# Another order for the first quarter of a fused attention and gated MLP kernel

## The chip, the cores and the metric

The program runs on one core of a Trainium2 chip. A core has a matrix engine (PE, which also has a queue for loading weights, PEld), a vector engine (DVE), a scalar engine (ACT), GpSimd (POOL) and a queue engine (SP) that here only issues transfers. Each engine takes its own instructions strictly in the order in which the program lists them, and waits at the first one whose inputs are not there. The metric is the device time of one execution in microseconds (us), as the median of several runs.

## The reference

Attention with a bucket mask, and then a gated MLP without a nonlinearity:

```python
def _attn_ref(q, k, v, proj):            # q, k, v: (4, 8, 768, 64), proj: (64, 6)
    q_bits = np.einsum('bhsd,dk->bhsk', q, proj) > 0        # 6 bits per token
    k_bits = np.einsum('bhsd,dk->bhsk', k, proj) > 0
    mask = q_bucket[:, :, :, None] == k_bucket[:, :, None, :]  # buckets made of the bits
    scores = np.where(mask, q @ k.T / sqrt(64), -1e9)
    attn = softmax(scores)
    return attn @ v
def _moe_ref(x, w_a, w_b, w_out):        # x: (3072, 512), d_ff = 1536
    return ((x @ w_a) * (x @ w_b)) @ w_out
```

The output of the attention, with its heads side by side, is the x of the MLP. Everything is float32 outside; inside the kernel most products run on 16-bit pieces, a high and a low one, of the float32 numbers.

## The kernel before, in words

The four batches are worked on one after the other, and each is cut into chunks of one or two blocks of 128 tokens (14 chunks). For a chunk there are eight or sixteen "query tiles" (`qtile`): scores of 128 queries against 768 keys on PE (`s`, L1136), their maximum on DVE (`mx`, L1156), a scale and a bias made from it (`sc`, `bias`, L1164 and L1168, on DVE or POOL), the exponential on ACT (`e`, L1177), a transpose of the result, and the product with v on PE (`av`). For the first chunk the transpose is made by PE (`et`); later it is a cast, a subtraction and a transfer that transposes (`at`).

Before the scores, q and k are prepared (`split`). A product of each with itself (`gram_q`, `gram_k`, L596) gives a bound, from which a power of two is made (`ps`, L534, then `ai`, L546 and L549). With it, the input is cut into a high part (L569 on DVE or L567 on ACT) and a low part (L670, DVE). High and low are transposed (`qt`, `kt`, L688, on PE for batch 0) and copied back (`trq`, `trk`, L560). Six hash bits are then computed from the transposed parts (`qb`, `kb`, L709 on PE; `neg`, L727 on ACT; `bits`, L730 on DVE) and written as extra rows beside the data (L736, L739 into `hp`), which are transposed and copied in a second round. A score needs both rounds of its q and its k. In batch 0 there are four pairs of heads for k (`rk` 0 to 3).

The MLP's weights arrive in float32, 512 KB each transfer (`to_f32`, L855), are put into an internal form by POOL or ACT (L868, L866), ACT (L876) and DVE (L884), and a bound is taken of them too (`gram_w`, L902). The first two chunks use float32 weights (L1363), the others 16-bit halves (L1371). The products with w_a and w_b are `ab`, their gated result is `g` (L1392, L1400, L1411, L1416), the last product is `o` (L1436). `ps_cx` (L768) gives the scale of a chunk's x. MLP work of a chunk stands between the query tiles of later chunks, so that PE has work while a score goes round DVE and ACT.

No scheduler runs: the program has 3,725 operations (`op`), numbered as the code makes them, and a table `ORDER` says in which order they are issued. A second table, `ENGINE_OF`, says on which engine those run that may run on several. `Plan.issue` only follows the two. Buffers are handed out in that order too: a tile that shares a buffer waits for the readers of the tile before it. There are two PSUM buffers for scores and the transposes `qt` and `kt`, and three smaller ones.

Of the kernel before, what the change touches and what calls it, by code (L numbers as in the profile page):

```python
# [426 lines left out]
def attention_moe(ctx: ExitStack, tc: tile.TileContext, q, k, v, proj, w_a, w_b, w_out, cst, out):  # L427
# [7 lines left out]
    op = plan.op  # L435
# [37 lines left out]
    pj = cp.tile([P, NBITS], F32, tag="pj", name="pj")  # L473
# [36 lines left out]
    pw = cp.tile([P, 4], F32, tag="pw", name="pw")  # L510
# [1029 lines left out]
```

## Time and profile before

| | |
|---|---|
| median of 3 runs | 891.82 us (891.47 to 892.02) |
| profiled execution | 892.21 us, of which the span from the first to the last instruction is 890.4 us |
| PE busy | 869.0 us, 98% of the span |
| DVE, ACT, POOL busy | 631.1, 565.9, 438.0 us |
| chain that ended last | 70% of the span PE; of it L1371 35%, L1436 17%, L1136 10%, L1205 8% |
| read and written in HBM | 37.82 MB, 6.29 MB |

Busy time is the sum of the time in which an engine had an instruction. The profile names, for idle time in front of an instruction, what ended it. PE is busy nearly always, so the places where it is not busy are few, and each has its own cause.

### The profile page before, as it was taken

The numbers are of one execution on the slowest core, as the hardware profiler recorded it, in microseconds if no ns is written. First come the engines' busy times: TensorE is split into PE (matmuls) and PEld (weight loads), VectorE is DVE, ScalarE is ACT, GpSimd is POOL, SyncE is SP. The second block draws the span as 40 slices with busy tenths as digits, with TensorE's granted clock in tenths as the row PEclk, the third lists the DMA queues.
The fourth block names the chain that finished last, engine by engine and source line by source line (L and its number), as shares of the span: only waits on it lengthen the run. The fifth ranks groups of instructions, "written<-read, shape, count | busy, mean of one in ns | idle before, by whom it ended". The sixth has DMA issues, their size and how long they took to land.

```text
span 890.4 us, 24299 instructions
## 1 busy us (share of the span) xinstructions
PE 869.0 (98%) x9761; PEld 672.4 (76%) x9761; DVE 631.1 (71%) x1461; ACT 565.9 (64%) x1116; POOL 438.0 (49%) x371
## 2 busy tenths in 40 slices
PE   5899999999999999999999999999999999999998
PEld 4798777878777777777777777777777777777775
DVE  7998999988876766767776775767778576643311
ACT  6887767766657777667666675667676466644222
POOL 2444456447426556554454565545556457544111
PEclk9999999999999999999999999999999999999999
DMA  9989996899979979998977787799987666745100
GB/s 328 302 268 260 173 167 148 155 191 191 196 144 191 162 162 168 172 224 154 185 137 155 149 170 158 131 195 173 200 170 138 125 149 125 144 90 103 30 24 24
DMA packets 430433, 145.31 MB, mean 163 GB/s; under 512 B 404080, under 2 KB 422640, under 8 KB 430320
## 3 DMA queue, kind: packets, MB, share of 16 engines
q1 hardware_dynamic: 430160, 143.76, 79.5%
q8 instruction: 76, 1.25, 0.6%
q14 instruction: 37, 0.30, 0.1%
q10 hardware_dynamic: 160, 0.00, 0.0%
HBM read 37.82 MB, written 6.29 MB: 50 GB/s over the span
## 4 chain that ended last, share of the span: by engine, by line
PE 70%; DVE 3%; issue 1%; ACT 0%; DVEq 0%; ACTq 0%
PE ab L1371 35%; PE o L1436 17%; PE s L1136 10%; PE av L1205 8%; DVE vh L569 0%; DVE g L1400 0%; PE qb L709 0%; DVE mx L1156 0%; PE kb L709 0%; DVE hp L736 0%; DVE hp L739 0%; DVE ai_q L549 0%; DVE osb L569 0%; DVE kt L670 0%; PE ps_cx L768 0%
## 5 line engine op out<-in xcount | busy, mean ns | idle before, releaser
L1371 PE MATMUL ab<-xT,wz 128*128 128x256 f16 (+1 forms) x3456 | 377.2, 264 | 1.0 <-DVE g L1400 0.8
L563 POOL TENSOR_TENSOR a<-e,a 128x768 f16<-128x768 f32 x170 | 286.2, 1687 | 186.7 <-ACT a L560 84.0
L1371 PEld LDWEIGHTS <-wz 128*128 128x128 f16 x3456 | 310.4, 98 | 49.5 <-issue 1.5
L1177 ACT ACTIVATE e<-s,bias,sc 128x768 f32<-128x768 f32 x192 | 189.7, 988 | 110.3 <-DVE bias L1168 93.0
L1156 DVE TENSOR_REDUCE mx<-s 128x1 f32<-128x768 f32 x192 | 182.6, 953 | 53.2 <-PE s L1136 49.1
L1436 PE MATMUL o<-wz,g 128*128 128x512 f16 (+1 forms) x840 | 215.8, 392 | 0.2 <-DVE g L1400 0.2
L1416 POOL TENSOR_TENSOR g<-g,g 128x256 f16<-128x256 f32 x132 | 94.8, 718 | 191.1 <-ACT g L1411 185.5
L1136 PE MATMUL s<-trk,trq 76*128 76x384 f16 (+1 forms) x768 | 155.0, 327 | 2.4 <-ACT e L1177 1.8
L1400 DVE SCALAR_TENSOR_TENSOR g<-ab,ab,a 128x256 f32<-128x256 f32 x132 | 63.4, 480 | 105.1 <-ACT a L1392 87.2
L1205 PEld LDWEIGHTS <-at 128*128 128x128 f16 x3312 | 117.5, 98 | 16.5 <-issue 2.7
L1436 PEld LDWEIGHTS <-g 128*128 128x128 f16 x792 | 73.9, 98 | 68.7
L1392 ACT ACTIVATE a<-ab,ab 128x256 f32<-128x256 f32 x132 | 62.1, 470 | 99.5 <-PE ab L1371 86.6
L1205 PE MATMUL av<-vh,at 128*128 128x64 f16 x2208 | 121.9, 193 | 0.0
L1136 PEld LDWEIGHTS <-trq 76*128 76x128 f16 (+1 forms) x768 | 70.6, 98 | 44.1 <-issue 6.8
L1411 ACT CAST g<-g 128x256 f16<-128x256 f32 x132 | 53.0, 402 | 59.0 <-DVE g L1400 48.5
L560 ACT CAST a<-e 128x768 f16<-128x768 f32 x102 | 84.5, 829 | 3.0 <-DMA at<-a 1.2
L1205 PE MATMUL av<-vl,at 128*128 128x64 f16 x1104 | 62.4, 193 | 0.0
L1363 PE MATMUL ab<-xT,wz 128*128 128x128 f32 x384 | 49.4, 279 | 0.0
L560 DVE CAST a<-e 128x768 f16<-128x768 f32 x68 | 39.4, 580 | 14.0 <-ACT e L1177 14.0
L1363 PEld LDWEIGHTS ab<-xT,wz 128*128 128x128 f32 x384 | 46.2, 192 | 3.4 <-issue 2.2
L1168 DVE TENSOR_SCALAR bias<-mx,sc 128x1 f32<-128x1 f32 x181 | 38.8, 214 | 6.4
L1164 DVE TENSOR_SCALAR sc<-mx,cq 128x1 f32<-128x1 f32 x181 | 38.3, 211 | 4.8
(171 smaller groups left out, 793.7 us busy)
## 6 DMA issues: line engine op xcount, KB each, us to landing
rq<-in_q_dram SPq DMA_DIRECT2D x24, 256.0 KB, 3.5
rk<-in_k_dram SPq DMA_DIRECT2D x16, 384.0 KB, 3.9
wz<-in_moe_w_a_dram SPq DMA_DIRECT2D x12, 512.0 KB, 5.9
wz<-in_moe_w_b_dram SPq DMA_DIRECT2D x12, 512.0 KB, 5.0
wz<-in_moe_w_out_dram SPq DMA_DIRECT2D x12, 512.0 KB, 5.6
out_dram<-osb SPq DMA_DIRECT2D x24, 256.0 KB, 2.4
vr<-in_v_dram SPq DMA_DIRECT2D x12, 384.0 KB, 4.4
at<-a SPq DMA_TRANSPOSE x184, 3.6
```

The costliest lines, as they stand in the source:

```text
L560: {"ACT": nc.scalar.copy, "DVE": nc.vector.tensor_copy, "POOL": nc.gpsimd.tensor_copy}[e](out=out, in_=x)
L563: (nc.gpsimd if e == "POOL" else nc.vector).tensor_tensor(out=out, in0=x, in1=y, op=ALU.subtract)
L1136: nc.tensor.matmul(ps.t[:, jj, :HALF], lhsT=trq.t[rows, i, (2 * j + h) * nt + t], rhs=tr.t[rows, i, k0 : k0 + NT // 2].rearrange("p n s -> ...
L1156: lambda: nc.vector.tensor_reduce(out=mx.t[:, col], in_=halves(ps.t), axis=AX.XY, op=ALU.max, negate=True),
L1177: lambda: nc.scalar.activation(flat2(e.t), halves(ps.t), AF.Exp, bias=bias.t[:, col], scale=sc.t[:, col], accum_out=sm.t[:, u : u + 1],),
L1205: nc.tensor.matmul(av.t[:, u, :], lhsT=at.t[:, a + kt, :], rhs=w.t[:, h, kt, :], start=i == 0, stop=i == 3 * NT - 1,)
L1363: nc.tensor.matmul(pl.t[:, m, to], lhsT=wt32(m, cc, f), rhs=xt.t[:, cc * nt // NC, cc * nt % NC : cc * nt % NC + nt, :], start=cc == 0, st ...
L1371: nc.tensor.matmul(pl.t[:, m, to], lhsT=wt(m, wi, cc, f), rhs=xt.t[:, cc * nt // NC, xi, cc * nt % NC : cc * nt % NC + nt, :], start=i == ...
L1392: lambda a=a, pl=pl, gr=gr, sc_of=sc_of: nc.scalar.activation(a.t, pl.t[:, 0, :CH], AF.Copy, scale=sc_of(gr)),
L1400: lambda a=a, g32=g32, pl=pl, gr=gr, sc_of=sc_of: nc.vector.scalar_tensor_tensor(out=g32.t, in0=pl.t[:, 1, :CH], scalar=sc_of(gr + 1), in1 ...
L1416: lambda g=g, g32=g32, g_of=g_of: nc.gpsimd.tensor_tensor(out=g_of(g[1]), in0=g32.t, in1=g_of(g[0]), op=ALU.subtract),
L1436: nc.tensor.matmul(po[u].t.rearrange("p a b -> p (a b)"), lhsT=x()[:, us], rhs=w, start=f == 0 and i == 0, stop=f == NF - 1 and i == len(t ...
```

## The change

The first 1,100 places of `ORDER` hold the same operations in another order; behind them nothing moves. 1,078 of these places hold another operation than before. 108 operations run on another engine: 31 go from DVE to POOL, 24 from DVE to ACT, 20 from ACT to DVE, 17 from POOL to DVE, 8 from ACT to POOL and 8 from POOL to ACT. Among those from DVE to POOL are 18 pairs of scale and bias; four such pairs go back. One operation, the small constants, is given an input in the plan so that it may stand behind the loading of `proj`.

```diff
 ORDER = (
-    2, 1, 75, 11, 76, 4, 3, 77, 5, 78, 79, 80, 81, 0, 12, 13, 14, 15, 6, 282, 281, 9, 10, 84, 27, 16, 82, 17, 83, 18,
+    1, 2, 5, 11, 3, 12, 4, 75, 281, 76, 13, 77, 78, 79, 14, 15, 114, 9, 10, 80, 6, 0, 16, 27, 7, 28, 81, 17, 29, 84,
...
 ENGINE_OF = {
     "ACT": (
-        19, 20, 35, 36, 42, 58, 64, 67, 74, 83, 84, 90, 105, 107, 119, 128, 138, 140, 149, 157, 159, 166, 168, 176, 178,
+        16, 19, 20, 26, 42, 64, 74, 80, 83, 90, 107, 109, 111, 119, 121, 130, 138, 140, 147, 149, 159, 176, 178, 185, 187,
...
-    op("DVE", 0.4, pw_consts, -79, w=["pw"])
+    op("DVE", 0.4, pw_consts, -79, r=[("pj", 0), ("pj", 1)], w=["pw"])
```

The first place is PE between the first transposes of k and its second round, at 9 to 18 us of the trace. `kt_0_0` is pair 0, `kt_0_1` pair 1; loads of weights and repeats are left out. Before:

```order
L688 MATMUL kt_0_0_155<-identh,kt_0_0_140 128x128
...
L596 MATMUL gram_k_1_171<-rk_1_138 128x128
...
L534 MATMUL ps_k_1_191<-st_k_1_189,onesr 128x1
...
L709 MATMUL kb_0_199<-pjw_67,trk_0_168 128x12
...
L709 MATMUL qb_0_217<-pjw_68,trq_0_153 128x12
...
L596 MATMUL gram_k_3_235<-rk_3_233 128x128
...
L688 MATMUL kt_0_1_246<-identh,kt_0_1_212 128x128
...
L534 MATMUL ps_k_3_267<-st_k_3_242,onesr 128x1
...
L688 MATMUL kt_0_0_278<-identh,hp_77 128x128
```

And now:

```order
L688 MATMUL kt_0_0_182<-identh,kt_0_0_137 128x128
...
L596 MATMUL gram_k_3_208<-rk_3_206 128x128
...
L688 MATMUL kt_0_1_217<-identh,kt_0_1_202 128x128
...
L534 MATMUL ps_k_3_232<-st_k_3_230,onesr 128x1
...
L709 MATMUL kb_0_235<-pjw_67,trk_0_195 128x12
...
L709 MATMUL qb_0_254<-pjw_68,trq_0_180 128x12
...
L596 MATMUL gram_k_2_275<-rk_2_250 128x128
...
L688 MATMUL kt_0_0_283<-identh,hp_77 128x128
```

The hash products of pair 0 (`kb_0`, `qb_0`) now stand behind the transposes of pair 1, and a product of pair 2 stands before the second round of pair 0.

The second place is PE around the first two scores, at 19 to 29 us. Before:

```order
L688 MATMUL qt_0_0_328<-identh,hp_76 128x128
...
L534 MATMUL ps_k_2_342<-st_k_2_339,onesr 128x1
...
L534 MATMUL ps_q_0_350<-st_q_0_348,onesr 128x1
...
L688 MATMUL kt_0_1_360<-identh,hp_77 128x128
...
L1136 MATMUL s_0_0_1_0_388<-trk_0_168,trq_0_153 128x384
...
L902 MATMUL gram_w_403<-wz 128x128
...
L596 MATMUL gram_v_0_423<-v_0_346 128x128
...
L1136 MATMUL s_0_0_0_0_433<-trk_0_168,trq_0_153 128x384
...
L688 MATMUL kt_0_2_439<-identh,kt_0_2_383 128x128
```

And now:

```order
L688 MATMUL qt_0_0_345<-identh,hp_76 128x128
...
L534 MATMUL ps_k_2_354<-st_k_2_331,onesr 128x1
...
L596 MATMUL gram_v_2_361<-v_2_323 128x128
...
L534 MATMUL ps_q_0_374<-st_q_0_341,onesr 128x1
...
L1136 MATMUL s_0_0_1_0_380<-trk_0_195,trq_0_180 128x384
...
L688 MATMUL kt_0_1_395<-identh,hp_77 128x128
...
L902 MATMUL gram_w_409<-wz 128x128
...
L1136 MATMUL s_0_0_0_0_432<-trk_0_195,trq_0_180 128x384
...
L688 MATMUL kt_0_2_442<-identh,kt_0_2_388 128x128
```

A product of v stands before the first score, and the second round of pair 1 (`kt_0_1` from `hp`) has moved behind it.

The third place is ACT in the second chunk, at 74 to 84 us, around the exponential `e_0_1_1_0`; `wz` are weights on their way to the internal form. Before:

```order
L1177 ACTIVATE e_0_3_0_0_1165,sm_0_1004<-s_0_3_0_0_1087,bias_0_951,sc_0_949 128x768
L866 ACTIVATE wz<-wz 128x1024
L560 CAST a_1_0_2_1_0_1171<-e_0_2_1_0_1065 128x768
L1392 ACTIVATE a_2_1190<-ab_2_1106 128x256
L876 ACTIVATE wz<-wz 128x1024
L1177 ACTIVATE e_0_1_1_0_1249,sm_0_1004<-s_0_1_1_0_1218,bias_0_951,sc_0_949 128x768
```

And now:

```order
L1177 ACTIVATE e_0_2_1_0_1136,sm_0_938<-s_0_2_1_0_1027,bias_0_905,sc_0_903 128x768
L567 ACTIVATE qt_3_0_1144<-rq_0_720,ai_q_0_1077 128x8x64
L866 ACTIVATE wz<-wz 128x1024 x2
L1177 ACTIVATE e_0_1_1_0_1169,sm_0_938<-s_0_1_1_0_1147,bias_0_905,sc_0_903 128x768
L1392 ACTIVATE a_2_1176<-ab_2_1071 128x256
```

The weight step L876 no longer stands directly before this exponential; two earlier ones of L866 do.

## Rows read from the trace of the kernel before

**Rows 1.** The page: span, and busy time of each engine.
```profile
span 890.4 us, 24299 instructions
...
PE 869.0 (98%) x9761; PEld 672.4 (76%) x9761; DVE 631.1 (71%) x1461; ACT 565.9 (64%) x1116; POOL 438.0 (49%) x371
```

**Rows 2.** Waits of PE: line <- releaser: us in total, times, longest.
```profile
PE gram_q L596 <- DMA rq<-in_q_dram: 4.0, 1, 4.0
...
PE s L1136 <- ACT e L1177: 1.8, 4, 0.6
PE ps_cx L768 <- ACT e L1177: 1.5, 1, 1.5
```

**Rows 3.** Five stretches: length, then busy us of PE, PEld, DVE, ACT, POOL, clock.
```profile
0.00:22.30 22.30, 12.30 (x133) 10.83 (x134) 16.11 (x51) 14.38 (x20) 5.14 (x8) 1.00 0.94 327
22.30:41.40 19.10, 16.88 (x186) 13.54 (x183) 18.64 (x43) 15.14 (x20) 9.20 (x9) 1.00 0.99 300
41.40:230.00 188.60, 186.19 (x2316) 152.93 (x2316) 170.69 (x364) 137.29 (x248) 97.72 (x84) 1.00 0.93 195
230.00:245.00 15.00, 13.51 (x152) 9.90 (x150) 13.57 (x29) 8.89 (x18) 7.05 (x6) 1.00 0.96 207
245.00:890.40 645.40, 640.13 (x6989) 485.21 (x6984) 412.04 (x978) 390.20 (x811) 318.88 (x264) 1.00 0.75 143
```

**Rows 4.** Timeline to 29 us: start, us, engine, instruction, [idle before].
```profile
9.66 1.46 PE L688 MATMUL kt<-identh,kt 128*128 128x128 f16 x12
...
12.50 2.18 ACT L876 ACTIVATE wz<-wz 128x1024 f32<-128x1024 f32 x2
...
12.66 0.49 PE L709 MATMUL kb<-pjw,trk 128*128 128x12 f16 x12 [0.31 <-ACT trk L560]
...
15.30 0.20 ACT L727 COPY neg_k<-kb 128x72 f32<-128x72 f32 x1
...
17.84 0.93 ACT L567 ACTIVATE kt<-rk,ai_k 128x768 f16<-128x768 f32 x1
...
18.92 0.94 DVE L560 COPY trk<-kt 128x1536 f16<-128x1536 f16 x1
...
20.82 1.01 ACT L560 COPY trq<-qt 128x1024 f16<-128x1024 f16 x1
...
21.93 1.44 PE L688 MATMUL kt<-identh,hp 128*128 128x128 f16 x12 [0.38 <-ACT trq L560]
...
23.17 1.48 PE L1136 MATMUL s<-trk,trq 76*128 76x384 f16 x4
...
24.45 1.91 PE L902 MATMUL gram_w<-wz 128*128 128x128 bf16 x16
...
28.24 0.83 PE L688 MATMUL kt<-identh,kt 128*128 128x128 f16 x12
28.91 1.08 PE L902 MATMUL gram_w<-wz 128*128 128x128 bf16 x16
```

**Rows 5.** The same columns as rows 3, for two stretches before 28 us.
```profile
16.40:21.90 5.50, 4.06 (x46) 3.76 (x46) 5.33 (x13) 5.33 (x8) 1.87 (x1) 1.00 1.01 346
21.90:28.00 6.10, 6.07 (x42) 4.79 (x43) 5.72 (x12) 4.21 (x5) 3.16 (x3) 1.00 1.02 345
```

**Rows 6.** Timeline around 82 us.
```profile
80.58 1.16 ACT L876 ACTIVATE wz<-wz 128x1024 f32<-128x1024 f32 x1 [3.44 <-DMA wz<-in_moe_w_b_dram]
...
82.75 0.81 PE L1136 MATMUL s<-trk,trq 76*128 76x384 f16 x4 [0.48 <-ACT e L1177]
```

**Rows 7.** The bias of a query tile (L1168): duration in ns, shortest/median/longest.
```profile
L1168 DVE TENSOR_SCALAR bias<-mx,sc x181: 212/214/217, 26.8 to 815.9; 128x1 f32<-128x1 f32 x181
L1168 POOL TENSOR_SCALAR bias<-mx,sc x11: 259/260/1280, 29.8 to 207.6; 128x1 f32<-128x1 f32 x11
```

**Rows 8.** The page's groups: maximum and exponential of a query tile.
```profile
L1177 ACT ACTIVATE e<-s,bias,sc 128x768 f32<-128x768 f32 x192 | 189.7, 988 | 110.3 <-DVE bias L1168 93.0
L1156 DVE TENSOR_REDUCE mx<-s 128x1 f32<-128x768 f32 x192 | 182.6, 953 | 53.2 <-PE s L1136 49.1
```

**Rows 9.** Timeline around 231 to 236 us.
```profile
231.53 1.64 POOL L563 TENSOR_TENSOR a<-e,a 128x768 f16<-128x768 f32 x1
231.54 1.69 DVE L739 TENSOR_SCALAR hp<-bits_k 128x72 f16<-128x72 f32 x1
...
235.24 0.27 PE L768 MATMUL ps_cx<-identb,cxs 128*128 128x128 bf16 x2 [1.49 <-ACT e L1177]
```

176 rows, old and new, of tables (ENGINE_OF, ORDER) are left out of this document.

## Prediction, made before the changed kernel ran

> **What bounds the kernel now.** I read the page first. PE is busy 869.0 us of a span of 890.4 us [rows 1], so whatever the change does, it can only win or lose in the 21.4 us in which PE is idle, or in PE's own speed. The profiled execution took 892.21 us, 1.8 us more than its span and 0.39 us above the median of the runs, 891.82 us; I make the sum against the profiled one and take the difference off the median.
>
> Next, the five stretches [rows 3]: length minus PE's busy time is PE's idle time. It is 10.0 us until 22.3 us, 2.22 us until 41.4 us, 2.41 us from there to 230 us, 1.49 us in the 15 us that follow, and 5.27 us in the remaining 645.4 us. The change reorders what runs until about 240 us, so the last 5.27 us are out of its reach unless another timing at 245 us is carried on, and 16.1 us are in reach. Of these, 4.0 us are the wait for the first transfer [rows 2]; whichever of q or k comes first, some transfer has to land. About 12 us remain to be won, and 8 of them lie before 41 us.
>
> Until 41.4 us DVE is the fuller engine: 16.11 us of 22.3 and 18.64 us of 19.1 [rows 3]. PE waits there for small results that go round DVE and ACT. From 41.4 us on PE is at 186.19 of 188.6 us and always has MLP work between the scores; its waits are single events, most of them a score that waits for an exponential (1.8 us in 4 places, [rows 2]).
>
> **The clock.** The granted clock reads 1.00 in every stretch [rows 3, 5], yet twelve transposes of the same shape took 1.44 us at 21.93 us and 0.83 us at 28.24 us, and sixteen products of the same shape 1.91 us at 24.45 us and 1.08 us at 28.91 us [rows 4]. So PE ran at its lower level (1.2 GHz) until about 28 us and at the higher (2.4 GHz) after. Before the rise, PE was busy 6.07 of 6.10 us; in the stretch before that, 4.06 of 5.50 us, it did not rise [rows 5]. A denser PE in the first 22 us may bring the rise earlier.
>
> **The change, part one: until the first score (row by row with durations of the trace).** Now k is loaded and measured before q. Both scales are ready by about 7.3 us. The high parts of q and k then both go to ACT, one behind the other: 0.93 us for k [rows 4] and, by columns, an estimated 0.65 us for q. The low part of k then ends on DVE near 10 us, and its transposes start at about 10.4 us, against 9.66 us before [rows 4]: 0.7 us late. The hash products `kb` now stand behind the transposes of pair 1 and come near 15.4 us, against 12.66 us: 2.7 us late. This costs little: before, their result lay until ACT, busy with two weight steps of 2.18 us together, made the negated bits at 15.30 us [rows 4]; now that step comes at about 15.9 us. So the second round is 0.6 us late. Its copy of k goes from DVE (0.94 us) to ACT (about 1.43 us), in front of the copy of q, which starts at about 22.1 us instead of 20.82 us [rows 4]. But the second transposes of pair 1, 1.44 us on PE before the first score, have moved behind it. The first score thus comes at 23.2 us, against 23.17 us [rows 4]. Nothing is won at this point; but PE has meanwhile done a product of v that before stood at 35 us, and owes the transposes of 1.44 us.
>
> What PE does on the way is denser: from 13.9 us to 21.9 us I count 7.5 us of work in 8.0 us (transposes 1.46 + 1.44 + 1.05, hash products and bounds about 1.5, four products of 0.6 to 0.84). By [rows 5] that should bring the rise of the clock to about 21 to 22 us. Then score, transposes, weight product and score after 23.2 us take about 3.5 us (0.8 + 0.83 + 1.08 + 0.8) and not about 6.2 us (1.48 + 1.44 + 1.91 + 1.41): 2.7 us of PE time. Most of this is not kept: the next transposes wait for DVE's low part of pair 2, which by DVE's queue ends near 27.8 us; they ran at 28.24 us before [rows 4], so 0.4 us is left. Following DVE's queue and PE in this way to the fourth score, PE has the work that it had done by 41.4 us done by 40.75 us. Term one: -0.65 us. Bounds: -2.5 us if all the clock gives is kept, +0.5 us if the clock rises no earlier.
>
> **Part two: 41.4 to 230 us.** PE is idle for 2.41 us there [rows 3]. The clearest case is the score at 82.75 us: it waits 0.48 us for an exponential, which stood on ACT behind a weight step that had itself waited 3.44 us for a transfer [rows 6]. In the new order that step is no longer in front of the exponential, so the wait goes. For the others I laid PE's rows of both orders end to end and counted the PE work between a score and the first PE instruction that waits for its exponential. Before, it is under 3.5 us in 10 of 49 cases and 2.86 us at the least; now in 4 of 50, and 3.35 us at the least. The shortest way round is 0.95 us of maximum, 0.43 us of scale and bias on DVE, 0.99 us of exponential [rows 7, 8], and about 0.3 us between the engines: 2.7 us. So the new order has more slack at the tight places. Two others get tighter: the transposes of the first chunk's output now follow the last `av` by 0.7 us of other PE work, and the first MLP product follows these transposes by 0.65 us, where 0.68 and 0.6 us of DVE and ACT work and the hops lie between; I charge 0.5 us for both. DVE is freed: it loses 18 operations net, a pair of scale and bias being 0.43 us each [rows 7]. I let two thirds of the 2.41 us go: -1.6 us. Bounds: -2.4 us and, if new waits take the place of the old, 0.
>
> **Part three: the end of the reordered part.** The 1.49 us at 235.24 us [rows 9] stand where the order is already as before. `ps_cx` there needs a buffer that an exponential still reads, and that one is late because two DVE instructions of the hash rows took 1.69 us beside a POOL subtraction of 1.64 us [rows 9]. The same instructions meet again; I leave it at 0, bounds -1.49 and +1.5 us. What is won before it can be lost here if PE arrives earlier and DVE does not.
>
> Sum: -0.65 - 1.6 + 0 = -2.25 us, 889.96 us for a profiled execution like this one and 889.6 us for the median.
>
> **A cost that speaks against it.** Moved to POOL, a bias takes 260 ns instead of 214, but up to 1,280 ns [rows 7]. Fourteen pairs more go there on balance. The Trainium skill, GPSIMD Engine Reference, section 1 (Specifications), says that GpSimd shares its SBUF interfaces with VectorE, so that it contends with DVE instructions that run in a 2-port mode or have two SBUF inputs. The 1.69 us beside 1.64 us agree with that. By that rule the moved pairs take some DVE time back; by the medians of rows 7 they free 6.0 us of DVE. This is the second rival.
>
> **Rivals.**
> 1. No change that can be measured. The first score comes no earlier (23.2 us), the clock's gain drowns in DVE's queue, and for every wait removed after 41.4 us another order makes a new one. For it: DVE is at 18.64 of 19.1 us until 41.4 us, and I found the start to be a draw. Against it: the longer distances of part two. About -0.3 us: 891.5 us.
> 2. Slower: the pairs on POOL. A pair that stands behind POOL's own work takes up to 1.28 us per instruction [rows 7], 2.6 us in place of 0.56 us. The way round a score is then 0.95 + 2.6 + 0.99 + 0.3 = 4.8 us, and with a distance of 3.35 to 3.5 us PE waits about 1.4 us. If that hits half of the four tight places, it is 2.7 us with nothing won before: 894.5 us. It decides where POOL is in a weight step or subtraction when the maximum ends. For it: 11 pairs on POOL before, and among them such a long one. Against it: POOL is busy only 97.72 of 188.6 us [rows 3].
> 3. More than forecast: all 2.41 us go, and the 1.49 us at 235 us too: -4.5 us, 887.3 us.
>
> **Chances.** Forecast 0.52, rival 1 0.22, rival 2 0.16, rival 3 0.10. The forecast's own range is 887.5 to 891.4 us, from the bounds of parts one and two together, a little drawn in. The range for 8 in 10 reaches into rivals 1 to 3: 887.0 to 893.2 us. A measurement of this kernel can tell about 0.2%, 1.8 us, from no change, so 890.0 us and below counts as faster. Of the forecast's 0.52 I put 0.38 there and 0.14 at no change; rival 3 is faster; rival 1 is 0.20 no change and 0.02 slower; rival 2 is 0.15 slower and 0.01 no change. Together: faster 0.48, same 0.35, slower 0.17.
>
> **What would show it.** In the new profile the first score should start near 23.2 us, with `kt` transposes before it already at 0.83 us if the clock has risen; the idle time of PE until 41.4 us should be about as before or larger, in a shorter time. Waits of `s` for `e` after 41.4 us should be under 0.8 us in total; a wait for POOL's `bias` in their place would show rival 2. `ps_cx` should still wait about 1.5 us. I am wrong if the first score comes before 21 us or after 25 us, or if PE's idle time after 41.4 us grows.

## The result and the profile after

The changed kernel is slower: 903.01 us median of 6 runs (899.37 to 904.78) against 892.34 us of the kernel before on the same chips (891.47 to 894.23), a ratio of 1.0111 with an interval of 1.0088 to 1.0135. Forecast were 889.6 us and a range that ends at 893.2 us. The profiled execution took 900.43 us, with a span of 898.6 us: 8.2 us more than [rows 1].

PE's busy time has not changed in sum, 869.07 us for 869.01, so the difference in span is idle time of PE. (Two effects of the clock stand against each other in that sum: it rises earlier at the start, and it falls once near 90 us, see below.) The five stretches of the kernel after, which answer to [rows 3] (length, then busy us of PE, PEld, DVE, ACT, POOL, and the granted clock):

```profile
0.00:22.30 22.30, 11.92 (x138) 9.80 (x139) 15.21 (x53) 14.32 (x19) 4.36 (x9) 0.92 0.93 326
22.30:41.40 19.10, 17.72 (x209) 15.15 (x208) 18.66 (x41) 16.12 (x24) 10.49 (x15) 0.91 0.89 305
41.40:230.00 188.60, 177.95 (x2153) 145.99 (x2151) 160.56 (x315) 135.06 (x238) 102.89 (x104) 0.99 0.93 187
230.00:245.00 15.00, 13.29 (x212) 10.39 (x210) 12.78 (x32) 9.56 (x22) 5.57 (x5) 1.00 1.06 176
245.00:898.60 653.60, 648.18 (x7061) 490.77 (x7058) 421.00 (x992) 393.71 (x818) 322.43 (x267) 1.00 0.80 144
```

Length minus busy time of PE gives 10.38, 1.38, 10.65, 1.71 and 5.42 us, against 10.0, 2.22, 2.41, 1.49 and 5.27 us before. Everything is lost between 41.4 and 230 us: 8.24 us, where the forecast had 1.6 us to win. No other engine is near its limit there: DVE is busy for 160.56 of 188.6 us, less than before, and POOL, which has more to do now, for 102.89 us.

PE's waits between 45 and 245 us, first of the kernel before and then of the one after (total us, times, longest):

```profile
PE ps_cx L768 <- ACT e L1177: 1.5, 1, 1.5
PE s L1136 <- ACT e L1177: 1.4, 3, 0.6
PE s L1136 <- DVE bits_q L730: 0.3, 1, 0.3
```

```profile
PE s L1136 <- DMA trq<-hp: 3.0, 1, 3.0
PE av L1205 <- DMA at<-a: 2.0, 2, 1.1
PE ps_cx L768 <- ACT e L1177: 1.6, 2, 0.8
PE qb L709 <- DMA trq<-qt: 1.5, 1, 1.5
PE s L1136 <- DVE bits_q L730: 1.1, 1, 1.1
PE ab L1363 <- DVE g L1400: 0.9, 1, 0.9
PE s L1136 <- ACT e L1177: 0.7, 2, 0.4
```

Scores wait half as long for exponentials as before, as forecast. But 6.5 us are now waits for transposing transfers (`trq`, `at`), where there were none, and waits for DVE rows have grown from 0.5 to 3.1 us. The queue of these transfers, SP, tells a part of why. Some of what it waited for in the same stretch, before and after (L855 loads weights, L1098 is the transfer that transposes `at`, L679 the one for q and k):

```profile
SPq L1098 <- PE av L1205: 14.1, 12, 2.4
SPq L1098 <- POOL a L563: 11.6, 7, 3.4
...
SPq L855 <- DVE wz L884: 6.1, 2, 3.9
```

```profile
SPq L855 <- DVE wz L884: 19.9, 5, 9.1
SPq L1098 <- POOL a L563: 15.8, 10, 4.6
SPq L1098 <- POOL bias L1168: 9.0, 6, 2.8
...
SPq L679 <- DVE wz L884: 6.2, 1, 6.2
```

A weight transfer (L855) may go only when DVE has read the weights that lie in its buffer (L884). (The weights come as 64-bit floats, so that 128x512 of them are the 512 KB of a transfer; L866 or L868, L876 and L884 make 32-bit floats of them.) SP now waits 19.9 us in 5 places for such steps, where it waited 6.1 us in 2, and everything behind them in the queue waits too. The last line is no such case: that L679, at 47.13 us, needs hash rows that DVE had written at 47.10 us, just before L884. All waits of SP together have not grown, 118.4 us before and 111.8 us after; what counts is what stands behind them. The longest case can be followed row by row (start, us). SP in the kernel after:

```profile
65.97 2.23 SPq L1098 DMA_TRANSPOSE at<-a  x1
77.43 0.81 SPq L855 DMA_DIRECT2D wz<-in_moe_w_b_dram  x2
78.38 1.68 SPq L1098 DMA_TRANSPOSE at<-a  x1
80.17 1.01 SPq L855 DMA_DIRECT2D wz<-in_moe_w_out_dram  x2
81.63 1.68 SPq L679 DMA_TRANSPOSE trq<-hp  x1
```

SP issued nothing from 68.2 to 77.43 us. DVE in the meantime:

```profile
71.44 1.65 DVE L739 TENSOR_SCALAR hp<-bits_q 128x48 f16<-128x48 f32 x1
73.01 1.01 DVE L972 SCALAR_TENSOR_TENSOR vl<-v,v_ai,vh 128x768 f16<-128x768 f32 x1
73.94 0.20 DVE L1147 TENSOR_SCALAR cq<-ai_q,ai_k 128x1 f32<-128x1 f32 x1
74.06 0.95 DVE L1156 TENSOR_REDUCE mx<-s 128x1 f32<-128x768 f32 x1
...
75.42 3.07 DVE L884 SCALAR_TENSOR_TENSOR wz<-wz 128x1024 int32<-128x1024 int32 x2
```

The weight step (the first of the two rows of L884) had its input at 70.4 us, from POOL, but stands behind the rows above it; before, its input came from ACT at 68.36 us, and it ran at 68.43 us. The hash rows for `trq<-hp` were written by 73.1 us. Their transfer was issued at 81.63 us, behind two pairs of weight transfers and a transfer of `at`, and PE waited for it:

```profile
90.71 1.46 PE L1136 MATMUL s<-trk,trq 76*128 76x384 f16 x4 [2.97 <-DMA trq<-hp]
```

Before, the same transfer was issued 3.3 us earlier, and its score started without a wait:

```profile
78.31 4.04 SPq L679 DMA_TRANSPOSE trq<-hp  x1
90.55 0.82 PE L1136 MATMUL s<-trk,trq 76*128 76x384 f16 x4
```

From issue to landing it took about as long both times, 8.8 us (landed at 87.12 us) and 9.0 us (at 90.66 us), so what came late is the issue. The stall cost more than its 2.97 us. The granted clock around it:

```profile
25.60:90.46 64.86, 58.54 (x612) 50.27 (x610) 56.80 (x113) 50.85 (x84) 29.92 (x37) 1.00 0.87 247
90.46:93.87 3.41, 3.16 (x13) 2.66 (x14) 3.18 (x5) 0.70 (x2) 0.42 (x1) 0.50 1.06 349
```

At half clock (1.2 GHz), the score above took 1.46 us and not 0.82, and sixteen products L1363 2.86 us, where sixteen at 70.28 us took 1.95: 1.5 us more.

To compare many kernels, I lay their PE work over that of the kernel before: each PE row counts with the step that its line has there at the higher clock, and the table says how much later (+) the same sum of work is done than before. All are single profiles, worked out from the traces:

| run | at 45 us | 95 | 130 | 170 | 250 | end |
|---|---|---|---|---|---|---|
| changed kernel | -2.95 | +3.51 | +4.59 | +5.07 | +7.90 | +8.3 |
| the same again (e12) | -1.23 | +3.83 | +5.13 | +7.23 | +10.71 | +11.1 |
| e3: new to 53 us, then old | -0.97 | +4.07 | +4.49 | +4.69 | +4.67 | +5.2 |
| e9: new to 130 us, then old | -0.84 | +2.28 | +4.72 | +3.93 | +3.94 | +4.3 |
| e4: old to 53 us, then new | -0.27 | +6.02 | +7.08 | +8.58 | +11.55 | +11.6 |
| e1: weight step earlier | -0.85 | +0.44 | +3.78 | +4.24 | +7.63 | +8.1 |
| e6: and four transfers earlier | -0.55 | +0.76 | +5.13 | +7.09 | +10.20 | +10.6 |
| e13: and 23 transfers by readiness | -1.45 | +0.31 | +0.56 | +0.95 | +3.30 | +3.7 |
| e14: e6 with readers later | -1.91 | +0.26 | +4.93 | +6.79 | +13.85 | +14.3 |

The new start leads by about 1 us at 45 us on average, over ten profiles; behind it the changed order loses 11 to 12 us by 250 us, about half of it before 95 us (6.5 and 5.1 us in its two profiles) and the rest in smaller steps. Where the loss before 95 us is mended, as in e1 and e6, more is lost later.

### The profile page after: what moved, and what is told of

It is laid out like the page before. It is cut to its first block, busy times and chain, and to the rows that moved or that the text cites. A ratio compares the mean times of both kernels' runs of the same rounds, so it can differ in the third digit from the quotient of the medians.

```text
span 898.6 us, 24300 instructions
## 1 busy us (share of the span) xinstructions
PE 869.1 (97%) x9761; PEld 672.1 (75%) x9761; DVE 628.2 (70%) x1429; ACT 568.8 (63%) x1120; POOL 445.7 (50%) x399
## 4 chain that ended last, share of the span: by engine, by line
PE 84%; DVE 7%; DMA 6%; issue 2%; ACT 1%; POOL 0%; SPq 0%; ACTq 0%; DVEq 0%; POOLq 0%
PE ab L1371 37%; PE o L1436 19%; PE s L1136 12%; PE av L1205 10%; PE ab L1363 3%; DMA at<-a 2%; DVE mx L1156 1%; DMA wz<-in_moe_w_a_dram 1%; DMA trq<-hp 1%; DMA wz<-in_moe_w_out_dram 1%; PE av L1190 1%; DMA trq<-qt 1%; DVE hp L739 1%; PE qb L709 0%; DVE g L1400 0%
## 5 line engine op out<-in xcount | busy, mean ns | idle before, releaser
L563 POOL TENSOR_TENSOR a<-e,a 128x768 f16<-128x768 f32 x169 | 284.0, 1685 | 168.0 <-ACT a L560 78.5
L560 ACT CAST a<-e 128x768 f16<-128x768 f32 x105 | 86.8, 828 | 5.5 <-DMA at<-a 2.2
L1363 PEld LDWEIGHTS ab<-xT,wz 128*128 128x128 f32 x384 | 47.9, 195 | 8.0 <-issue 4.7
L1363 PE MATMUL ab<-xT,wz 128*128 128x128 f32 x384 | 50.8, 282 | 0.9 <-DVE g L1400 0.9
L1168 DVE TENSOR_SCALAR bias<-mx,sc 128x1 f32<-128x1 f32 x167 | 35.8, 214 | 5.9
L1164 DVE TENSOR_SCALAR sc<-mx,cq 128x1 f32<-128x1 f32 x167 | 35.3, 211 | 4.3
```

Of the source, the lines that this page charges most:

```text
L560: {"ACT": nc.scalar.copy, "DVE": nc.vector.tensor_copy, "POOL": nc.gpsimd.tensor_copy}[e](out=out, in_=x)
L563: (nc.gpsimd if e == "POOL" else nc.vector).tensor_tensor(out=out, in0=x, in1=y, op=ALU.subtract)
L1363: nc.tensor.matmul(pl.t[:, m, to], lhsT=wt32(m, cc, f), rhs=xt.t[:, cc * nt // NC, cc * nt % NC : cc * nt % NC + nt, :], start=cc == 0, st ...
```

## The experiments

All were timed beside the kernel before. Medians and ratios:

| run | median us | ratio (interval) |
|---|---|---|
| e1 weight step earlier | 900.84 | 1.0088 (1.0062 to 1.0114) |
| e2 new order, old engines | 932.32 | 1.0448 (1.0432 to 1.0464) |
| e3 new start, old rest | 897.31 | 1.0058 (1.0046 to 1.0070) |
| e4 old start, new rest | 902.09 | 1.0110 (1.0096 to 1.0123) |
| e5 four transfers earlier | 900.54 | 1.0098 (1.0080 to 1.0116) |
| e6 both of e1 and e5 | 900.95 | 1.0098 (1.0083 to 1.0113) |
| e7 new to 33 us, old rest | 894.54 | 1.0027 (1.0017 to 1.0037) |
| e8 pairs back | 912.98 | 1.0247 (1.0226 to 1.0268) |
| e9 new to 130 us, old rest | 898.93 | 1.0081 (1.0067 to 1.0095) |
| e10 old order, new engines | 928.87 | 1.0410 (1.0396 to 1.0424) |
| e11 new to 40 us, old rest | 896.74 | 1.0053 (1.0039 to 1.0066) |
| e12 changed kernel again | 902.75 | 1.0114 (1.0097 to 1.0131) |
| e13 transfers by readiness | 897.00 | 1.0064 (1.0052 to 1.0077) |
| e14 readers later | 910.82 | 1.0204 (1.0186 to 1.0221) |
| e15 both | 910.86 | 1.0212 (1.0195 to 1.0229) |

**Where it is lost (e3, e4, e7, e9, e11).** The table of places is cut: the first 260 (150, 200, 600) places of one order, and then the remaining operations in the sequence of the other, each part with its own engine choices.

```diff
 ORDER = (          # e3: 260 places of the changed order, then the old one
...
     208, 136, 189, 139,
-    190, 341, 342, 349, 210,
+    226, 243, 341, 146, 147, 148,
...
```

e3: 

> The changed order and engines for the first 260 places (to about 53 us), and behind them what is left in the order and on the engines of before. Theory Q: the start itself wins 2 us (the cumulated PE work led by 2 to 3 us until 64 us) and nothing is lost later, 889.5 to 891 us. Theory P: the choices of the start are part of the loss, 893 to 896 us. Theory S: all of the loss shows, 900 us or more.

e4: 

> The order and engines of before for the first 260 places (to about 53 us), and behind them what is left in the changed order on the changed engines. Theory Q: without the won start and with the held transfer queue, 902 to 906 us. Theory P: 898 to 903 us. Theory S: back to 892 us.

e7: 

> The changed order and engines for the first 150 places only (to about 33 us), then what is left in the order and on the engines of before. In the run with 260 places PE led the kernel before by 0.7 to 1.5 us until 55 us, then lost 5.3 us in 10 us at the joint (waits of 0.65, 0.57 and 1.09 us, then the clock at half from 62.46 to 69.28 us). Theory J (that loss is of the joint alone): with a joint elsewhere 889.5 to 892 us. Theory S (the new start is itself worth nothing, or leaves debts that are paid at about 60 us): 893 us or more.

e11: 

> The changed order and engines for the first 200 places (to about 40 us), then what is left as before; the joint lies between those of the runs with 150 and 260 places. Theory J (the start wins 0.5 to 1 us when nothing is lost at the joint): 889.5 to 892 us. Theory S (the start wins nothing that is kept): 893 to 898 us.

e9: 

> The changed order and engines for the first 600 places (to about 130 us), then what is left as before. Theory R (the changed order loses everywhere behind the start, some 5 us between 45 and 130 us and some 4 to 5 us between 130 and 245 us, because transfers and the three small engines are late for their readers all along): about half of the loss, 896 to 898.5 us. Theory B (the loss is one block at 67 to 100 us and what follows from it): the whole loss stays, 901 to 904 us. Theory T (the loss comes from the last part, behind 130 us): back to 892 us.

e3, 897.31 us, lies between theories P and S. Theory S of the first runs, a start that itself costs, falls with e4: with the old start all of the loss is there, 902.09 us, and its profile has the changed kernel's waits again, among them 2.06 us for `trq` at 93.10 us. e9 is just above theory R's 896 to 898.5 us, and its profile shows what R says: +5.6 us between 45 and 130 us, and then, in the old order, nothing more (+4.72 to +3.94). In e3 too the old order loses little from 95 us on (+4.07 to +4.67). But no joint was clean. e3 lost 6.3 us between 55 and 65 us, to waits of 0.65, 0.57 and 1.09 us and the lower clock from 62.46 to 69.28 us; e11 lost 3.20 us in one wait for an exponential at 50.40 us and 1.7 us of clock behind it; e7 1.93 us at 38.12 us. e7 and e11 have no lead at 45 us at all (+1.24 and +0.38 us). By their times e7 and e11 came out as their theory S had it, 894.54 us (893 or more) and 896.74 us (893 to 898), and against theory J. The start's lead is there in the profiles of the longer pieces, but in no kernel was it kept; whether it is lost only at the joints was not separated.

**Order or engines (e2, e8, e10).**

```diff
 ENGINE_OF = {      # e8: of the 22 changed scale and bias pairs, 18 back to DVE and 4 to POOL
     "DVE": (
+        125, 135, 154, 173, 182, 211, 253, 584, 601, 618, 865, 881, 889, 906, 952, 960, 976, 993,
...
     "POOL": (
+        228, 245, 737, 968,
...
```

e2: 

> The changed order of places, with every operation on the engine it had before. Theory Q (what counts is the order in which DVE and the transfer queue meet): it stays slow, 898 to 908 us, since the weight step still stands behind the same DVE rows. Theory P (engine choices): back to 892 us or under. Theory S: stays at 900 us or more.

e8: 

> The changed order, with the 22 scale and bias pairs whose engine changed put back on the engine they had (18 to DVE, 4 to POOL); all other engine choices as changed. Theory P (pairs on POOL lengthen the way round a score): 3 us or more faster than the changed kernel, 900 us or less. Theory Q (DVE is the engine whose queue makes the transfers late, and 14 pairs more are 6 us of DVE time): slower than the changed kernel, 904 to 910 us.

e10: 

> The order of before, with every operation on the engine that the change gives it. Theory M (an order and its engine choices fit only each other; the new order with the old engines took 932.3 us): clearly slower than before, 900 to 930 us. Theory P (moving work off DVE is the good half of the change): 892 us or less.

Theory P falls three times over. With the pairs back the kernel is 10 us slower than with them on POOL, more than even theory Q had said; the old engines under the new order cost 29 us more than the new ones (against theory Q too, which had allowed 908 us), and the new engines under the old order 37 us more than the old ones (theory M). In e2 and e10 PE's waits are again those of scores for exponentials, 8.5 us in 9 places and 9.0 us in 8 between 45 and 245 us. Here an order and its engine choices fit only each other.

**The queue of transfers (e1, e5, e6, e13).**

```diff
 ORDER = (          # e1: the POOL step 363 and the DVE step 365 of one weight group
-    108, 375, 252, 348, 409, ..., 236, 363, 365, 368, 370,
+    108, 363, 375, 252, 365, 348, 409, ..., 236, 368, 370,
 ORDER = (          # e5: 555 is trq_2_0[0]; 605, 942 and 989 likewise
-    368, 370, 381, 377, ..., 228, 415, 555, 382,
+    368, 370, 555, 381, 377, ..., 228, 415, 382,
 ORDER = (          # e13: one of 23; 240 is at_1_0_1_1_0
-    384, 371, 395, 394, ..., 258, 896, 240, 594,
+    384, 371, 240, 395, 394, ..., 258, 896, 594,
```

e1: 

> The changed order, with two operations of the weight path put earlier in the table and nothing else: the POOL step L868 and the DVE step L884 of the weight group whose buffer the transfer at 77.43 us waits for. Theory Q (the transfer queue stood still from 68 to 77 us behind that one load, so that the transposing transfer of the score at 90.71 us came 9 us late): the wait of 2.97 us goes, the clock no longer falls behind it and the score that waits 1.15 us at 111.85 us waits less, so 3.5 to 5 us faster than the changed kernel, 898 to 899.5 us. Theory P (the engine choices, above all scale and bias on POOL, make the loss all along): no change, 902 to 903.5 us. Theory S (the new first 50 us cost it): no change either.

SP issued that load at 71.74 us and not at 77.43, and the wait at 90.71 us was gone, with the fall of the clock: at 95 us e1 is only 0.44 us behind. But the next late tile took its place at once:

```profile
100.36 0.35 PE L1205 MATMUL av<-vh,at 128*128 128x64 f16 x6 [2.61 <-DMA at<-a]
```

The median, 900.84 us, is 2 us under that of the changed kernel, within the scatter of either, and between theory Q (898 to 899.5 us) and theories P and S (902 to 903.5 us).

e5: 

> The changed order, with four of its transposing transfers put earlier in the table, past other transfers only (trq_2_0[0] past five, at_2_0_2_1_0 and at_4_1_1_0_0 past two each, trq_4_1[1] past one as far as its buffer allows); nothing moves on the four computing engines. In the changed kernel each of the four landed 0.04 us before the PE row that then started. Theory Q (the loss is transposing transfers that stand behind other transfers in their one queue): the waits at 90.71 and 236.36 us go (2.97 and 0.89 us, and 1.7 us of lower clock behind the first), 3 to 5.5 us faster than the changed kernel, 897.5 to 900 us. Theory R (the changed order leaves too little PE work between a tile and its reader, wherever the transfers stand): the waits move to other tiles, within 1.5 us of 903 us.

e6: 

> The four transfers earlier as in the run before, and the two operations of the weight path earlier as in the first experiment. Theory Q: both add up, 894 to 898 us. Theory R: no better than 900 us, with new waits of PE for DMA rows between 100 and 240 us.

e5 came out between the theories, e6 as theory R had it: the waits aimed at shrank or went, and others came (in e6 2.10 us for `at` at 100.16 us with the clock at half from 100.68 to 104.09 us, and 1.97 us for `at` at 211.21 us). Mending single places did not make the kernel measurably faster.

e13: 

> The run with four transfers and the weight step earlier (900.95 us), and on top of it 23 transposing transfers between 45 and 245 us put in front of other transfers by up to six places, wherever its profile shows that their data was there before the transfer ahead of them could start; the computing engines keep their order. Theory Q (the order of the one transfer queue is the cause): the waits of PE for DMA rows behind 45 us go, some 4 us, and the clock's loss at 100.68 us, 895 to 897.5 us. Theory E (the three small engines deliver late, the queue only passes it on): 899 to 902 us, with waits of PE for DVE, ACT or DMA rows of other tiles.

Against e6, 23 transfers were moved in the queue, and nothing on the computing engines. The stretch from 45 to 245 us (length, then busy us of PE, PEld, DVE, ACT, POOL, clock), before, after and in e13:

```profile
45.00:245.00 200.00, 196.15 (x2438) 159.92 (x2438) 180.69 (x383) 143.03 (x261) 104.47 (x89) 1.00 0.93 194
```

```profile
45.00:245.00 200.00, 187.96 (x2332) 153.50 (x2332) 170.81 (x343) 141.44 (x254) 106.25 (x105) 0.99 0.94 184
```

```profile
45.00:245.00 200.00, 192.56 (x2383) 157.33 (x2382) 174.36 (x352) 145.39 (x261) 109.49 (x108) 1.00 0.96 193
```

PE idles 3.85, 12.04 and 7.44 us. What is left in e13:

```profile
PE ps_cx L768 <- ACT e L1177: 1.4, 2, 0.8
PE s L1136 <- DVE bits_q L730: 1.1, 1, 1.1
PE av L1205 <- DMA at<-a: 1.1, 2, 0.8
PE ab L1363 <- DVE g L1400: 1.1, 1, 1.1
PE s L1136 <- DVE x_mx L549: 0.8, 1, 0.8
PE qb L709 <- DMA trq<-qt: 0.7, 1, 0.7
PE s L1136 <- DMA trq<-hp: 0.4, 1, 0.4
```

PE's waits for transposing transfers fell from 5.7 us in e6 (6.5 us in the changed kernel) to 2.2 us, and SP's waits to load weights behind L884 from 15.6 us (19.9 us) to 7.1 us. The ratio fell from 1.0098 in e6 to 1.0064, and the intervals do not touch: 3.0 us for the order of the one queue alone, 4.0 us by the medians. Theory Q is shown as a part of the cause, a third or somewhat more of the 9 us that e6 loses. It is not all that the queue may cost: a tile still lies 2.45 us in it once its data is ready, for 3.34 us in e6 and 1.73 us in the kernel before (means over the tiles of scores, as in the table of the next section). What is left of PE's waits is mostly for DVE (3.3 us) and ACT (1.4 us), so that theory E is right in part as well, though its time, 899 to 902 us, is not.

**Readers later (e14, e15).**

```diff
 ORDER = (          # e14: one of 38 groups of av on PE; 224 is av_1_0[1]
-    241, 583, 224, 501, 502, ..., 431, 433,
+    583, 501, 502, ..., 431, 241, 224, 433,
```

(241 is another `av` and moves too. Their order among themselves stays. The kernels that ran move 38 groups and not 40.)

e14: 

> The same run as base (900.95 us), and 40 groups of av on PE (L1205) between 80 and 240 us put later by 2.2 us of other PE work on average; the transfers keep their places. Theory E (tiles come late by 1 to 3 us, wherever they stand): waits of PE for `at` go, 3 us or more faster, 895 to 898 us. Theory F (an av put later frees its buffers later, so the next transfers and casts start later, and the waits come back): 899 to 905 us.

e15: 

> The 23 transfers by readiness and the readers later, as far as buffers allow (2.0 us on average). Theory Q and theory E together: 892 to 896 us. Theory F: 899 us or more.

Theory F, by more than it said: e14 is 10 us slower than its base e6, and e15 14 us slower than its base e13. In e14 the waits for `at` did go, from 4.7 us in 3 places to 0.6 us in one, but those for `trq` grew from 1.0 to 3.6 us. And the queue now waits longer for `av`, which frees the buffers: 26.2 us in 17 places in e14, 17.4 us in 10 in e6 (SP's waits of e14, then of e6):

```profile
SPq L1098 <- PE av L1205: 26.2, 17, 4.7
```

```profile
SPq L1098 <- PE av L1205: 17.4, 10, 3.6
```

and at the end of the reordered part `ps_cx` waits 3.10 us for an exponential at 249.09 us. Putting the readers later is no way out here, since they hold the buffers that the next tiles need. That this is all of the 10 us is not shown.

**The changed kernel again (e12).** 

> The changed kernel again, as it is. If the gains and waits of its first profile are typical, PE leads the kernel before by 2 to 3 us at 45 us and the score after the transposing transfer near 90 us waits 2 to 3 us again. If the start is a draw from execution to execution, the lead lies anywhere between -3 and +1.5 us, as in the other runs with this start, and the single waits lie elsewhere with about the same sum; 900 to 905 us in both cases.

 902.75 us. The lead at 45 us is 1.23 us this time; the score near 90 us waits again (2.22 us at 91.00 us, clock at half from 90.81 to 94.22 us), and so do `bits_q` at 112 us (1.14 us) and `qb` at 186 us (1.52 us). So the large waits come back with the order and are not chance; how large the lead is does differ from execution to execution. In ten profiles with the changed start up to 53 us or more, the lead at 45 us is 1.13 us on average, from 2.95 us ahead to 0.41 us behind.

None of the kernels tried is faster than the kernel before.

## Why the prediction was wrong

**Part one (until the first score, -0.65 us) held on average.** The first transposes of k came at 10.19 us (forecast 10.4), `kb` at 14.70 us (15.4), the first score at 21.84 us (23.2; in other profiles up to 24.45). The lead at 45 us is 1.13 us on average over ten profiles; the 2.95 us of this one lie beyond the bound of 2.5 us. (In the forecast's sum of 7.5 us of work from 13.9 us on, the items named add to 7.85 us at the least; the step does not turn on it.) Its steps in the kernel after, to be laid beside [rows 4]:

```profile
10.19 1.44 PE L688 MATMUL kt<-identh,kt 128*128 128x128 f16 x12
13.97 0.84 PE L688 MATMUL kt<-identh,kt 128*128 128x128 f16 x12 [1.63 <-DVE kt L670]
21.84 1.16 PE L1136 MATMUL s<-trk,trq 76*128 76x384 f16 x4 [0.68 <-ACT trq L560]
22.79 1.49 PE L688 MATMUL kt<-identh,hp 128*128 128x128 f16 x12
26.79 0.83 PE L688 MATMUL kt<-identh,kt 128*128 128x128 f16 x12 [0.17 <-ACT e L1177]
```

The clock did rise earlier, but not for good at 21 to 22 us: twelve transposes took 0.84 us at 13.97 us, 1.49 us again at 22.79 us, and 0.83 us from 26.79 us on; the granted clock is 1.00 from 25.60 until 90.46 us. In e3 and e6, with the same start, it rose at 21.50 and 22.17 us and stayed up for 40 us and more. The forecast of this step was thus off by about 4 us in this profile and right in others, and the sum did not turn on it, since most of the clock's gain had been written off.

**Part two (41.4 to 230 us, -1.6 us) is the step that failed, and with it the sum.** What it looked at came as forecast: waits of scores for exponentials fell from 1.4 to 0.7 us. What it did not look at decided. It counted the PE work between a score and the row that waits for its exponential, along maximum, scale and bias, and exponential. The way goes on: a cast, a subtraction, SP's queue, a transfer and then `av`. And besides it runs the way of the weights, which hold up the same queue. I laid these ways out for every tile of scores that a transfer transposes, for the 44 tiles before and 42 after whose transfer is issued up to 245 us (one profile of each). From the end of the score to its `av`, and the four parts of that, mean us:

| | score to `av` | score until data is ready | held in SP's queue once ready | issue to landing | landed until used |
|---|---|---|---|---|---|
| before | 25.36 | 14.10 | 1.73 | 4.22 | 5.30 |
| after | 27.79 | 15.62 | 3.21 | 4.76 | 4.20 |

The new order does give more room, 2.4 us per tile, which fits what the forecast had seen. But 3.5 us more are used up: 1.5 us on DVE, ACT and POOL, 1.5 us in SP's queue and 0.5 us in the transfer. Most of the first comes at one step. The subtraction, the last row before the transfer, starts 2.42 us after the cast has ended, where it started 1.22 us after it (2.37 us in e12, and still 2.49 us in e13); 31 of the 42 subtractions run on POOL, as 33 of 44 did. No run moved the subtractions alone, so what this costs PE is not shown. Before, every transposed tile of this stretch, scores' and keys' included, had landed at least 0.4 us before its reader; after, six landed 0.04 us before PE took them.

The bounds of this step were wrong too: -2.4 to 0. The idle time that is there bounds what can be won; nothing in the rows bounded what can be lost, since any row of a new order may stand behind a row that is late. I had put rival 2, the only slower one, at 2.7 us and at a single mechanism, and neither was right.

**Part three (0) held in size.** PE idles 1.71 us in that stretch, where it idled 1.49 us. The DVE row and the POOL subtraction of [rows 9] met again, as forecast: L739 took 1.68 us at 239.47 us (it is this one row that takes the time, before as after, and not two). But `ps_cx` behind them waits 0.81 us at 243.13 us, and the rest is 0.89 us for a transfer of `at` at 236.36 us. That the sum came out is luck.

**Rival 2 (pairs on POOL) is not the cause.** ACT did wait longer for POOL's bias, as the rival had it (45 to 245 us, before and after):

```profile
ACT e L1177 <- POOL bias L1168: 3.2, 4, 2.0
ACT e L1177 <- POOL bias L1168: 9.0, 9, 2.7
```

But PE's waits for exponentials fell all the same, and in e8 the pairs back on DVE made the kernel 10 us slower, with the subtractions still 2.22 us behind the casts. That DVE lacked the time for them fits this; it was not tested by itself.

**Rivals 1 and 3** fall with the result.

**What stays open.** Of what the changed order loses behind 45 us, the order of the one queue explains 3 to 4 us by the runs of e13 against e6 (6 of 10.8 us by their two profiles, but e6's was the slowest of its runs and e13's the fastest). The rest shows in e13 as waits for DVE and ACT rows and as tiles that are ready late, most of them at the subtraction. Which sequence on which of the three small engines makes them late, and what it costs, was not tested. And the lead of the start was nowhere kept long enough to be timed by itself.

## What to carry to other kernels

Where an order is changed, walk the transfer queue like an engine: for each transfer, when its data is ready, what stands ahead of it that may itself wait, and when its reader comes. In a kernel whose main engine is 98% busy, the idle time that is left bounds the gain of a new order and not its loss; price the other side by how many readers have little room. Order and engine choices are one solution: the engine choices of one order, put under the other, cost 29 and 37 us here.

## What the runs showed of the hardware

- A DVE row beside a POOL subtraction: L739 took 1.65 us at 71.44 us, beside 1.70 us of L563 on POOL that began at 71.34 us; before, the same row took 0.18 us at 71.19 us, with POOL idle. The Trainium skill, GPSIMD Engine Reference, section 1 (Specifications), says that GpSimd shares its SBUF interfaces with VectorE and contends with DVE instructions in a 2-port mode or with two SBUF inputs; the rows agree with the sharing. Which of the two conditions this row with its one input meets, no run here shows.

```profile
71.34 1.70 POOL L563 TENSOR_TENSOR a<-e,a 128x768 f16<-128x768 f32 x1
```

The row before:

```profile
71.19 0.18 DVE L739 TENSOR_SCALAR hp<-bits_q 128x48 f16<-128x48 f32 x1
```

- Waits of PE and the clock in a busy stretch: around the end of waits of 2.97, 2.22, 3.20 and 2.10 us (changed kernel, e12, e11, e6) the granted clock fell to half for a while; behind waits of 2.61 us (e1, at 100.36 us), 2.32 us (e15, at 120.52 us) and 1.86 us (e9, at 90.99 us) it stayed at 1.00. A stall of that size cost 1.5 us more than it lasted in the changed kernel, and in others nothing more.
- The same transfer does not land in the same time in another order: `at_4_1_1_0_0` landed 2.11 us after its issue had ended before the change, and 4.79 us after, directly behind a load of k of 384 KB; `trq_4_1[1]` 1.48 and 3.36 us.
- Runs of some kernels scatter more: those of the kernel before lay within 4 us (890.34 to 894.23), those of the changed order within 5.4 us, of e1 within 8.7 us and of e8 within 8.2 us, but those of e10, 37 us slower than before, within 2.5 us. Why is not shown.
